# A decode layer on one core: the first MLP layer by wide matmuls on four column strips, gelu and silu by tanh

## The chip, the core and the metric

The kernel runs on one core of a Trainium2 chip. The metric is the device time of one execution in microseconds (us). TensorE is written PE in the profile (PEld for its weight loads), VectorE is DVE, ScalarE is ACT, GpSimd is POOL, and SyncE, which issues most of the DMAs, is SP.

## What is computed

Four batch rows, one token each. The token is layer-normed once; the result goes through attention over the last 1024 positions of a cache (32 query heads, 8 key/value heads, head size 128) and through an MLP with its own layer norm; the two are multiplied, the MLP's output after a silu, and added to the input.

```python
x = A_x                                   # (4, 1, 512)
xn = layernorm(x)
q = xn @ wq                               # 32 heads of 128
s = softmax(q k^T * 128**-0.5) v @ wo     # k, v: last 1024 rows of the caches
y = layernorm(xn)
h = gelu(y @ w1 + b1)                     # tanh form; w1 is (512, 1792)
g = silu(h @ w2 + b2)                     # w2 is (1792, 512)
out = x + s * g
```

All inputs are bf16. With four rows nearly all the work is moving weights and caches: 16 MB of K and V, 4 MB each of `wq` and `wo`, 1.75 MB each of `w1` and `w2`.

## The kernel before

The program is written out as a list of operations for each engine. `_Program.add` (L28) appends an operation with what it depends on to one engine's list, `dma` (L33) does it for a transfer, and `emit` (L52) writes each engine's list in that order, with a semaphore wait ahead of an operation where a dependency lies on another engine. So the order of the `add` calls is the order of each engine's queue, and an operation that waits holds up all that stands behind it on its engine.

The work is staged as follows.

- **Loads.** SP issues everything large in one order: `wq` in two halves with the first K heads between them, all K heads (`load_k`, L206), then V(0), `w1`, V(1), `w2`, V(2) to V(7) (`load_v`, L211), then `wo` in six pieces (L459): three of two heads each, one of one head, and the last head as three quarters and one quarter. V(g) takes the buffer of K(g), so its load waits until the transposes of K(g) are done. The small `x`, `b1`, `b2` go on ACT's queue. POOL builds constants: ones, an identity, selection masks, the mask `negm`, and clears `xT`.
- **Norms and queries.** DVE computes both layer norms. `f_xy` (L348) transposes the two normed inputs to `xT` (padded to 32 columns a chunk) and `yT` (4 columns a chunk). `f_q` (L362) computes the queries with `xT` as the loaded side and `wq` as the moving side: 32 matmuls of 512 columns, four at a time on four strips of 32 columns of PE's array (`tile_position`).
- **K phase.** For each of 32 units (4 per head): `T(n)` (L278) transposes eight 128x128 blocks of K on PE (L284), DVE copies the result to `kt_buf` (L290), and `S(n)` (L293) computes scores with eight narrow matmuls (L303), `LAG` = 8 units later. At the end of a head ACT takes the exponent into `P_buf` (L311).
- **V phase.** For each head `PV(g)` (L315) does 32 matmuls (L321) and one 512-column matmul with ones for the denominator (L327). `epilogue(g)` (L331) reduces and inverts the denominator and scales, on DVE. PV(g) waits for epilogue(g-2).
- **MLP.** It is put between heads by the loop that ends with the calls of `mlp1` to `mlp4`. `mlp1` (L391) follows PV(0): for each of 14 chunks of the hidden size, four matmuls with a block of `w1` as the loaded side (its columns 14 elements apart, L397) and 4 moving columns of `yT`, and one with a row of `b1` (L399). The hidden layer so stands transposed, 128 partitions by 56. ACT squares it (L404), DVE forms the cubic argument (L405, L407), ACT takes an exponent (L408); `mlp2` (L411, called after PV(1)) adds one, inverts and multiplies on DVE to give `hT`. `mlp3` (L418) does the second layer, 56 matmuls with blocks of `w2` as the loaded side (L424) and 4 with a row of `b2` (L426), then an exponent on ACT (L430); `mlp4` (L433, after PV(2)) makes the silu, `g_sb`, on DVE.
- **End.** After the last epilogue, `to_rows` (L462) brings the attention output into the order of `wo`'s rows (L470, L477), `wo(k, rows)` (L483) does 128 matmuls in six groups, one for each piece of `wo`, each waiting for its piece (L491). The sum is multiplied with `g_sb` (L517), transposed (L521), added to `x` (L523) and stored (L525).

Of the kernel before, what the change touches and what calls it, by code (L numbers as in the profile page):

```python
# [16 lines left out]
class _Program:  # L17
# [56 lines left out]
def bass_recurrent_scan__sliding_block_cached__mixer_channel_mlp__decode_kernel(  # L74
# [25 lines left out]
    F = B_w1.shape[1]  # L100
    FC = F // 128
# [6 lines left out]
    NKT = LAG + 2  # L108
    NB = 3
    SCALE = DH ** -0.5  # L110
    GELU_A = 1.5957691216057308
    GELU_K = 0.044715
    EPS = 1e-5
    NEG = -30000.0
# [1 line left out]
    sb = nc.alloc_sbuf_tensor  # L116
# [13 lines left out]
    x32 = sb([4, 512], F32)  # L130
# [5 lines left out]
    xn32 = sb([4, 512], F32)  # L136
    xn_bf = sb([4, 512], BF16)
    st2 = sb([4, 6], F32)
    mv2 = sb([4, 2], F32)
# [5 lines left out]
    ones_bf = sb([128, 128], BF16)  # L145
    ident = sb([128, 128], BF16)
# [4 lines left out]
    negm = sb([128, 512], BF16)  # L151

    xT = sb([128, 4, 32], BF16)
    yT = sb([128, 16], BF16)
    q_sb = sb([128, 2, 512], BF16)
    qT = sb([128, 128], BF16)
    b1_sb = sb([1, F], BF16)
    b2_sb = sb([1, D], BF16)
    sel = sb([128, 4, 32], BF16)
    OW = sb([128, 4, HKV * 4], BF16)  # L160
    hT = sb([128, FC * 4], BF16)

    OTb = sb([128, HKV * 16], BF16)
    den_sb = sb([128, HKV * 16], F32)
    rden = sb([128, HKV * 16], F32)

    u2_sb = sb([128, FC * 4], F32)
    t_sb = sb([128, FC * 4], F32)
    t2_sb = sb([128, FC * 4], F32)
    ge_sb = sb([128, FC * 4], F32)  # L170
    e1_sb = sb([128, FC * 4], F32)
    r_sb = sb([128, FC * 4], F32)

    ez_sb = sb([128, 16], F32)
    d1_sb = sb([128, 16], F32)
    rz_sb = sb([128, 16], F32)
    g_sb = sb([128, 16], F32)
    sg_sb = sb([128, 16], F32)
    o_bf = sb([16, 128], BF16)
# [5 lines left out]
    PS_Q, PS_H, PS_Z, PS_W = 0, 128, 192, 208  # L185

    pg = _Program(nc)
    add = pg.add
# [3 lines left out]
    d_b1 = pg.dma("act", "b1", lambda e: e.dma_start(  # L192
        b1_sb[0:1, :], B_b1.rearrange("(o n) -> o n", o=1)))
    d_b2 = pg.dma("act", "b2", lambda e: e.dma_start(
        b2_sb[0:1, :], B_b2.rearrange("(o n) -> o n", o=1)))

    def cache_rows(cache, g):

# [27 lines left out]
    for g in range(2, HKV):  # L226
# [5 lines left out]
    c_id = add("gp", lambda e: e.affine_select(  # L232
        ident[:, :], ones_bf[:, :], [[1, 128]], ALU.is_equal, 0.0,
        base=0, channel_multiplier=-1), c_1)
# [4 lines left out]
        sel[:, :, :], ones_bf[:, :], [[1, 4], [4, 32]], ALU.is_equal, 0.0,  # L239
        base=0, channel_multiplier=-1), c_1)  # L240
    c_xT = add("gp", lambda e: e.memset(xT[:, :, :], 0.0))
    c_z = add("gp", lambda e: e.memset(zero_bf[:, :], 0.0))
    c_neg = add("gp", lambda e: e.affine_select(
        negm[:, :], zero_bf[:, :], [[0, 32], [1, 4], [0, 4]], ALU.is_equal, NEG,
# [98 lines left out]

    v_xyT = None
# [3 lines left out]
    def f_xy(pe):  # L348
# [35 lines left out]
    for k in range(2):  # L384
        v_q = add("dve", lambda e, k=k: e.tensor_copy(
            bass.AP(qT, k * 64, [[128, 128], [16, 4], [4, 4], [1, 4]]),
            bass.AP(psK[1], k * 512, [[1024, 128], [32, 4], [1, 4], [128, 4]])), t_qT)

    mlp = {}

    def mlp1():  # L391
        def fn(pe):
            last = None
            for k in range(FC):
                o = psM[:, PS_H + k * 4:PS_H + (k + 1) * 4]
                for c in range(4):
                    pe.matmul(o, bass.AP(w1_sb, c * F + k, [[4 * F, 128], [FC, 128]]),  # L397
                              yT[:, c * 4:(c + 1) * 4], start=(c == 0), stop=False)
# [3 lines left out]
        h = psM[:, PS_H:PS_H + FC * 4]  # L402
        t = add("pe", fn, v_xyT, d_w1, d_b1)
        a = add("act", lambda e: e.activation(u2_sb[:, :], h, AF.Square), t)  # L404
        v = add("dve", lambda e: e.tensor_scalar(t_sb[:, :], u2_sb[:, :], GELU_K, 1.0,  # L405
                                                 op0=ALU.mult, op1=ALU.add), a)
        v = add("dve", lambda e: e.tensor_tensor(t2_sb[:, :], t_sb[:, :], h, ALU.mult), v)  # L407
        mlp["e"] = add("act", lambda e: e.activation(ge_sb[:, :], t2_sb[:, :], AF.Exp,  # L408
                                                     scale=-GELU_A), v)

    def mlp2():  # L411
        h = psM[:, PS_H:PS_H + FC * 4]
# [3 lines left out]
        mlp["h"] = add("dve", lambda e: e.tensor_tensor(hT[:, :], h, r_sb[:, :], ALU.mult), v)  # L416

    def mlp3():  # L418
        def fn(pe):
            last = None  # L420
            for c in range(4):
                o = psM[:, PS_Z + c * 4:PS_Z + (c + 1) * 4]
                for k in range(FC):
                    pe.matmul(o, w2_sb[:, k, c * 128:(c + 1) * 128], hT[:, k * 4:(k + 1) * 4],  # L424
                              start=(k == 0), stop=False)
                last = pe.matmul(o, b2_sb[0:1, c * 128:(c + 1) * 128], ones_bf[0:1, 0:4],  # L426
                                 start=False, stop=True)
            return last
        t = add("pe", fn, mlp["h"], d_w2, d_b2)
        mlp["ez"] = add("act", lambda e: e.activation(  # L430
            ez_sb[:, :], psM[:, PS_Z:PS_Z + 16], AF.Exp, scale=-1.0), t)

    def mlp4():  # L433
        v = add("dve", lambda e: e.tensor_single_scalar(d1_sb[:, :], ez_sb[:, :], 1.0, ALU.add),
                mlp["ez"])
        v = add("dve", lambda e: e.reciprocal(rz_sb[:, :], d1_sb[:, :]), v)
        mlp["g"] = add("dve", lambda e: e.tensor_tensor(
            g_sb[:, :], psM[:, PS_Z:PS_Z + 16], rz_sb[:, :], ALU.mult), v)

    NUN = HKV * NU  # L440
    for n in range(LAG, NUN + LAG):
# [137 lines left out]
```

## Time and profile before

| | |
|---|---|
| median of 4 runs | 77.22 us (77.1 to 77.3) |
| the profiled execution's own time | 77.23 us |
| its span in the profile | 75.3 us |
| granted PE clock, mean over the span | 0.803 |
| PE matmuls busy | 52.5 us (70%), 1107 of them |
| PE weight loads busy | 45.3 us (60%) |
| DVE busy | 38.4 us (51%) |
| ACT busy | 9.0 us (12%) |
| read from HBM | 28.85 MB |

The span runs from the first to the last instruction of the profiled execution; the time of a run also has what lies around it. A line of the page's groups names the kernel's line, the engine, the operation, what is written and read with shapes, and how often; then busy time and the mean of one in ns. In the timeline a row has start and length in us, and in square brackets how long the engine stood idle before it and what ended that. In the chain of work that ended last a row has start, length and what it was; "issue" is time in which the engine waited for nothing that the profile shows.

### The profile page before, as it was taken

The page shows a single profiled execution, that of the slowest core. Times are in us where ns is not written, and L with a number is a line of the kernel's source. Part 1 is how long each engine was busy: PE and PEld are TensorE (multiplying, and loading weights), DVE is VectorE, ACT ScalarE, POOL GpSimd, SP SyncE. Part 2 cuts the span into 40 slices and gives each one's busy share as a digit, 9 for nine tenths or more (in the row PEclk, how much of TensorE's full clock was granted, in tenths as well). Part 3 has the DMA queues.
Part 4 walks back from the last instruction along what each step waited for, and adds up shares of the span by engine and source line. Part 5 has one row for each costly group of instructions (what it writes and reads, how often), then busy time and mean ns, then how long its engine had stood idle before and what let it go on. Part 6 is the DMA issues. An engine that isn't in the chain of part 4 may idle for free.

```text
span 75.3 us, 2408 instructions
## 1 busy us (share of the span) xinstructions
PE 52.5 (70%) x1107; PEld 45.3 (60%) x1107; DVE 38.4 (51%) x84; ACT 9.0 (12%) x16; POOL 4.5 (6%) x13
## 2 busy tenths in 40 slices
PE   0000039974789979979968944999839999937960
PEld 0000039963269979969957933999639856806940
DVE  0778006894258979959975100000691687781010
ACT  0611000000270302303201520000200000000000
POOL 6970000000000000000000000000000000000000
PEclk9999999999999999999999996555555555555555
DMA  1899999998999999999999999999999999999600
GB/s 36 270 428 414 420 431 461 461 418 374 431 431 418 418 426 422 431 426 460 428 391 441 438 420 399 418 418 426 422 439 435 409 400 418 429 405 425 249 11 2
DMA packets 4213, 28.99 MB, mean 385 GB/s; under 512 B 486, under 2 KB 619, under 8 KB 1644
## 3 DMA queue, kind: packets, MB, share of 16 engines
q1 hardware_dynamic: 4160, 28.84, 92.1%
q8 instruction: 8, 0.13, 0.6%
q10 hardware_dynamic: 44, 0.01, 0.1%
q14 instruction: 1, 0.01, 0.0%
HBM read 28.85 MB, written 0.00 MB: 383 GB/s over the span
## 4 chain that ended last, share of the span: by engine, by line
DMA 36%; PE 34%; SPq 17%; DVE 5%; issue 4%
DMA wo_sb<-in_A_wo_dram 24%; PE psK L284 21%; SPq L459 16%; DMA kv_buf<-in_A_k_cache_dram 12%; PE psS L303 6%; DVE kt_buf L290 3%; PE psO L367 3%; PE psS L299 2%; DVE q_sb L373 1%; PE psK L379 1%; PE psM L491 1%; PE psK L352 1%; PE psS L521 1%; SPq L219 1%; SPq L212 0%
## 5 line engine op out<-in xcount | busy, mean ns | idle before, releaser
L284 PE MATMUL psK<-ident,kv_buf 128*128 128x128 bf16 x256 | 20.7, 233 | 12.2 <-DMA kv_buf<-in_A_k_cache_dram 10.7
L290 DVE COPY kt_buf<-psK 128x1024 bf16<-128x1024 bf16 x32 | 21.2, 691 | 8.4 <-PE psK L284 8.1
L284 PEld LDWEIGHTS psK<-ident,kv_buf 128*128 128x128 bf16 x256 | 16.6, 105 | 11.8 <-DMA kv_buf<-in_A_k_cache_dram 10.7
L303 PEld LDWEIGHTS psS<-qT,kt_buf 128*128 128x128 bf16 x256 | 9.4, 96 | 2.1 <-issue 1.2
L303 PE MATMUL psS<-qT,kt_buf 128*128 128x16 bf16 x256 | 10.4, 169 | 0.4 <-issue 0.4
L321 PEld LDWEIGHTS psO<-P_buf,kv_buf 128*128 128x128 bf16 x256 | 7.5, 103 | 2.1 <-issue 2.1
L321 PE MATMUL psO<-P_buf,kv_buf 128*128 128x16 bf16 x256 | 8.0, 174 | 0.2
L397 PE MATMUL psM<-yT,w_sb 128*128 128x4 bf16 x56 | 5.7, 204 | 2.1 <-issue 2.1
L311 ACT ACTIVATE P_buf<-psS 128x512 bf16<-128x512 f32 x8 | 4.8, 597 | 16.8 <-PE psS L303 16.8
L334 DVE TENSOR_REDUCE den_sb<-psS 128x16 f32<-128x512 f32 x8 | 5.5, 690 | 1.4 <-PE psS L327 1.2
L405 DVE TENSOR_SCALAR t_sb<-u_sb 128x56 f32<-128x56 f32 x1 | 0.2, 193 | 11.7 <-ACT u_sb L404 11.7
L397 PEld LDWEIGHTS psM<-yT,w_sb 128*128 128x128 bf16 x56 | 4.5, 153 | 2.5 <-issue 2.3
L327 PE MATMUL psS<-P_buf,ones_bf 128*128 128x512 bf16 x8 | 4.5, 561 | 0.0
L491 PE MATMUL psM<-OW,wo_sb 128*128 128x4 bf16 x128 | 3.9, 166 | 0.6 <-DVE OW L477 0.5
L491 PEld LDWEIGHTS psM<-OW,wo_sb 128*128 128x128 bf16 x128 | 3.7, 104 | 0.8 <-issue 0.6
L424 PE MATMUL psM<-hT,w_sb 128*128 128x4 bf16 x56 | 2.1, 167 | 1.4 <-DVE hT L416 1.4
L299 PE MATMUL psS<-negm,ind 128*128 128x512 bf16 x8 | 3.0, 380 | 0.0
L399 PE MATMUL psM<-ones_bf,b_sb 1*128 1x4 bf16 x14 | 3.0, 215 | 0.0
L424 PEld LDWEIGHTS psM<-hT,w_sb 128*128 128x128 bf16 x56 | 1.8, 105 | 1.9 <-DVE hT L416 1.9
L517 DVE TENSOR_TENSOR sg_sb<-psM,g_sb 128x16 f32<-128x16 f32 x1 | 0.2, 184 | 4.1 <-PE psM L491 4.1
L374 ACT ACTIVATE q_sb<-psO 128x512 bf16<-128x512 f32 x1 | 0.6, 597 | 13.5 <-PE psO L367 13.5
L337 DVE RECIPROCAL rden<-den_sb 128x16 f32<-128x16 f32 x8 | 2.0, 253 | 0.3
(63 smaller groups left out, 28.5 us busy)
## 6 DMA issues: line engine op xcount, KB each, us to landing
kv_buf<-in_A_k_cache_dram SPq DMA_DIRECT2D x8, 1024.0 KB, 20.7
kv_buf<-in_A_v_cache_dram SPq DMA_DIRECT2D x8, 1024.0 KB, 23.7
wq_sb<-in_A_wq_dram SPq DMA_DIRECT2D x2, 2048.0 KB, 11.4
w_sb<-in_B_w_dram SPq DMA_DIRECT2D x2, 1792.0 KB, 28.3
wo_sb<-in_A_wo_dram SPq DMA_DIRECT2D x3, 1024.0 KB, 24.8
wo_sb<-in_A_wo_dram SPq DMA_DIRECT2D x1, 512.0 KB, 21.4
wo_sb<-in_A_wo_dram SPq DMA_DIRECT2D x1, 384.0 KB, 18.0
wo_sb<-in_A_wo_dram SPq DMA_DIRECT2D x1, 128.0 KB, 17.9
```

Of the source, the lines that this page charges most:

```text
L284: last = pe.transpose(psK[n % NB][:, j * 128:(j + 1) * 128], kv_buf[:, g, u * UT + j, :], ident[:, :])
L290: cp[n] = add("dve", lambda e: e.tensor_copy(kt_buf[:, n % NKT, :], psK[n % NB][:, 0:1024]), t, sc.get(n - NKT))
L299: pe.matmul(psS[g % 2][:, 0:512], ind[:, :], negm[:, :], start=True, stop=False, skip_group_check=True)
L303: last = pe.matmul(psS[g % 2][:, c * 16:(c + 1) * 16], kt_buf[:, n % NKT, j * 128:(j + 1) * 128], qT[:, g * 16:(g + 1) * 16], start=False, ...
L311: ex[g] = add("act", lambda e: e.activation(P_buf[:, g, :], psS[g % 2][:, 0:512], AF.Exp, scale=SCALE), sc[n])
L321: last = pe.matmul(pso[:, 0:16], kv_buf[:, (HKV + g) % NS, c, :], P_buf[:, g, c * 16:(c + 1) * 16], start=(c == 0), stop=(c == NC - 1))
L327: den[g] = add("pe", lambda pe: pe.matmul(psS[g % 2][:, 0:512], ones_bf[:, :], P_buf[:, g, :], start=True, stop=True), ex[HKV - 2 + g % 2] ...
L334: v = add("dve", lambda e: e.tensor_reduce(den_sb[:, cs], bass.AP(psS[g % 2], 0, [[512, 128], [1, 16], [16, NC]]), AX.X, ALU.add), den[g])
L397: pe.matmul(o, bass.AP(w1_sb, c * F + k, [[4 * F, 128], [FC, 128]]), yT[:, c * 4:(c + 1) * 4], start=(c == 0), stop=False)
L424: pe.matmul(o, w2_sb[:, k, c * 128:(c + 1) * 128], hT[:, k * 4:(k + 1) * 4], start=(k == 0), stop=False)
L459: e.dma_start(wo_sb[:, g0:g1, i0:i1, :], wo_r[:, g0:g1, i0:i1, :]))))
L491: last = pe.matmul(psM[:, PS_W + c * 4:PS_W + (c + 1) * 4], wo_sb[:, g, i, c * 128:(c + 1) * 128], OW[:, i, g * 4:(g + 1) * 4], start=firs ...
```

## The change

The hidden layer is computed in rows instead of columns. `yT` is padded to 32 columns a chunk, like `xT`, and becomes the loaded side; `w1` becomes the moving side. Each of four column strips takes four of the 14 hidden chunks (the first chunks are 0, 4, 8 and 10, so two chunks are computed twice), 512 columns a matmul: 4 x 4 matmuls, and 4 more that add `b1` by a row of ones. The moving side reads `w1` with a step of 14 elements. The result stands in PSUM as 128 partitions (four strips of 32, of which four rows each are used) by 512.

Gelu is taken in its tanh form on tiles of 128x512: a square on ACT, one combined add-and-multiply on DVE, a tanh on ACT, then half of (tanh + 1) and a product on DVE. The tiles lie in buffers of `kt_buf`, which the K phase no longer needs, and the sums in `psK[0]`. Four transposes on PE and one DVE copy with a rearranged order bring it to `hT`.

The second layer is the same 56 blocks, with the loop over hidden chunks outside; its bias is one matmul ahead of them, with `b2` loaded as four rows of 128 and the identity's first four columns repeated four times as the moving side. Silu is taken by tanh too. `epilogue(0)` is moved ahead of `mlp1`. `x32` and `xn32` now lie inside `P_buf`, and POOL clears `yT`.

The core of the diff (declarations of tiles left out):

```diff
-    v_xyT = add("dve", lambda e: e.tensor_copy(yT[:, :], psK[1][:, 16:32]), t_xy)
+    v_xyT = add("dve", lambda e: e.tensor_copy(
+        yT[:, :, 0:4], psK[1][:, 16:32].rearrange("p (c b) -> p c b", c=4)), t_xy, c_yT)
...
+    K0 = (0, 4, 8, FC - 4)
+    def f32k(n):
+        return kt_buf[:, n, :].bitcast(F32)
+    hb = kt_buf[:, 4, 0:512]
+    h_ps = psK[0][:, 0:1024].bitcast(F32)
     def mlp1():
         def fn(pe):
             last = None
-            for k in range(FC):
-                o = psM[:, PS_H + k * 4:PS_H + (k + 1) * 4]
-                for c in range(4):
-                    pe.matmul(o, bass.AP(w1_sb, c * F + k, [[4 * F, 128], [FC, 128]]),
-                              yT[:, c * 4:(c + 1) * 4], start=(c == 0), stop=False)
-                last = pe.matmul(o, bass.AP(b1_sb, k, [[F, 1], [FC, 128]]), ones_bf[0:1, 0:4],
-                                 start=False, stop=True)
+            for c in range(4):
+                for s in range(4):
+                    pe.matmul(psK[0][32 * s:32 * s + 32, 0:1024].bitcast(F32), yT[:, c, :],
+                              bass.AP(w1_sb, c * F + K0[s], [[4 * F, 128], [1, 4], [FC, 128]]),
+                              start=(c == 0), stop=False, tile_position=(0, 32 * s))
+            for s in range(4):
+                last = pe.matmul(psK[0][32 * s:32 * s + 32, 0:1024].bitcast(F32),
+                                 ones_bf[0:1, 0:32],
+                                 bass.AP(b1_sb, K0[s], [[F, 1], [1, 4], [FC, 128]]),
+                                 start=False, stop=True, tile_position=(0, 32 * s))
             return last
...
-        t = add("pe", fn, v_xyT, d_w1, d_b1)
-        a = add("act", lambda e: e.activation(u2_sb[:, :], h, AF.Square), t)
-        v = add("dve", lambda e: e.tensor_scalar(t_sb[:, :], u2_sb[:, :], GELU_K, 1.0,
-                                                 op0=ALU.mult, op1=ALU.add), a)
-        v = add("dve", lambda e: e.tensor_tensor(t2_sb[:, :], t_sb[:, :], h, ALU.mult), v)
-        mlp["e"] = add("act", lambda e: e.activation(ge_sb[:, :], t2_sb[:, :], AF.Exp,
-                                                     scale=-GELU_A), v)
+        t = add("pe", fn, v_xyT, d_w1, d_b1, *[cp[n] for n in range(NUN - NB, NUN)])
+        a = add("act", lambda e: e.activation(f32k(0), h_ps, AF.Square), t)
+        v = add("dve", lambda e: e.scalar_tensor_tensor(f32k(1), f32k(0), 1.0 / GELU_K, h_ps,
+                                                        op0=ALU.add, op1=ALU.mult), a)
+        mlp["t"] = add("act", lambda e: e.activation(f32k(2), f32k(1), AF.Tanh,
+                                                     scale=GELU_C * GELU_K), v)
     def mlp2():
-        v = add("dve", lambda e: e.tensor_single_scalar(e1_sb[:, :], ge_sb[:, :], 1.0, ALU.add),
-                mlp["e"])
-        v = add("dve", lambda e: e.reciprocal(r_sb[:, :], e1_sb[:, :]), v)
-        mlp["h"] = add("dve", lambda e: e.tensor_tensor(hT[:, :], h, r_sb[:, :], ALU.mult), v)
+        v = add("dve", lambda e: e.tensor_scalar(f32k(3), f32k(2), 0.5, 0.5,
+                                                 op0=ALU.mult, op1=ALU.add), mlp["t"])
+        v = add("dve", lambda e: e.tensor_tensor(hb, f32k(3), h_ps, ALU.mult), v)
+        def fn(pe):
+            last = None
+            for t in range(4):
+                last = pe.transpose(psK[2][:, t * 128:(t + 1) * 128],
+                                    kt_buf[:, 4, t * 128:(t + 1) * 128], ident[:, :])
+            return last
+        t = add("pe", fn, v, cp[NUN - 1], cp[NUN - 2])
+        mlp["h"] = add("dve", lambda e: e.tensor_copy(
+            bass.AP(hT, 0, [[64, 128], [4, 16], [1, 4]]),
+            bass.AP(psK[2], 0, [[1024, 128], [32, 16], [1, 4]])), t)
     def mlp3():
         def fn(pe):
-            last = None
-            for c in range(4):
-                o = psM[:, PS_Z + c * 4:PS_Z + (c + 1) * 4]
-                for k in range(FC):
-                    pe.matmul(o, w2_sb[:, k, c * 128:(c + 1) * 128], hT[:, k * 4:(k + 1) * 4],
-                              start=(k == 0), stop=False)
-                last = pe.matmul(o, b2_sb[0:1, c * 128:(c + 1) * 128], ones_bf[0:1, 0:4],
-                                 start=False, stop=True)
+            last = pe.matmul(psM[:, PS_Z:PS_Z + 16], b2_sb[:, :],
+                             bass.AP(ident, 0, [[128, 4], [1, 4], [0, 4]]),
+                             start=True, stop=False, skip_group_check=True)
+            for k in range(FC):
+                s = min(k // 4, 2) if k < FC - 4 else 3
+                n = (k - K0[s]) * 16 + s * 4
+                for c in range(4):
+                    last = pe.matmul(psM[:, PS_Z + c * 4:PS_Z + (c + 1) * 4],
+                                     w2_sb[:, k, c * 128:(c + 1) * 128], hT[:, n:n + 4],
+                                     start=False, stop=(k == FC - 1), skip_group_check=True)
             return last
-        t = add("pe", fn, mlp["h"], d_w2, d_b2)
-        mlp["ez"] = add("act", lambda e: e.activation(
-            ez_sb[:, :], psM[:, PS_Z:PS_Z + 16], AF.Exp, scale=-1.0), t)
+        t = add("pe", fn, mlp["h"], d_w2, d_b2, c_id)
+        mlp["tz"] = add("act", lambda e: e.activation(
+            tz_sb[:, :], psM[:, PS_Z:PS_Z + 16], AF.Tanh, scale=0.5), t)
     def mlp4():
-        v = add("dve", lambda e: e.tensor_single_scalar(d1_sb[:, :], ez_sb[:, :], 1.0, ALU.add),
-                mlp["ez"])
-        v = add("dve", lambda e: e.reciprocal(rz_sb[:, :], d1_sb[:, :]), v)
+        v = add("dve", lambda e: e.tensor_scalar(sz_sb[:, :], tz_sb[:, :], 0.5, 0.5,
+                                                 op0=ALU.mult, op1=ALU.add), mlp["tz"])
...
     for g in range(HKV):
         PV(g)
         if g == 0:
+            epilogue(0)
             mlp1()
-        if g >= 1:
+        if g >= 2:
             epilogue(g - 1)
         if g == 1:
             mlp2()
             mlp3()
         if g == 2:
             mlp4()
```

More of the change, by code (lines that the diff above doesn't have):

```diff
@@ L110, in bass_recurrent_scan__sliding_block_cached__mixer_channel_mlp__decode_kernel @@
     SCALE = DH ** -0.5
-    GELU_A = 1.5957691216057308
+    GELU_C = 0.7978845608028654
     GELU_K = 0.044715
@@ L129, in bass_recurrent_scan__sliding_block_cached__mixer_channel_mlp__decode_kernel @@
     x16 = sb([16, 128], BF16)
-    x32 = sb([4, 512], F32)
+    x32 = P_buf[0:4, 4:6, :].rearrange("p g n -> p (g n)").bitcast(F32)
+    xn32 = P_buf[0:4, 6:8, :].rearrange("p g n -> p (g n)").bitcast(F32)
     st1 = sb([4, 6], F32)
@@ L135, in bass_recurrent_scan__sliding_block_cached__mixer_channel_mlp__decode_kernel @@
     rstd1 = sb([4, 1], F32)
-    xn32 = sb([4, 512], F32)
     xn_bf = sb([4, 512], BF16)
@@ L153, in bass_recurrent_scan__sliding_block_cached__mixer_channel_mlp__decode_kernel @@
     xT = sb([128, 4, 32], BF16)
-    yT = sb([128, 16], BF16)
+    yT = sb([128, 4, 32], BF16)
     q_sb = sb([128, 2, 512], BF16)
@@ L157, in bass_recurrent_scan__sliding_block_cached__mixer_channel_mlp__decode_kernel @@
     b1_sb = sb([1, F], BF16)
-    b2_sb = sb([1, D], BF16)
+    b2_sb = sb([4, 128], BF16)
     sel = sb([128, 4, 32], BF16)
     OW = sb([128, 4, HKV * 4], BF16)
-    hT = sb([128, FC * 4], BF16)
+    hT = sb([128, 64], BF16)
     OTb = sb([128, HKV * 16], BF16)
@@ L165, in bass_recurrent_scan__sliding_block_cached__mixer_channel_mlp__decode_kernel @@
     rden = sb([128, HKV * 16], F32)
[L167 to L176, printed above, removed]
+    tz_sb = sb([128, 16], F32)
+    sz_sb = sb([128, 16], F32)
     g_sb = sb([128, 16], F32)
@@ L184, in bass_recurrent_scan__sliding_block_cached__mixer_channel_mlp__decode_kernel @@
     psM = nc.alloc_psum_tensor("psM", [128, 512], F32)
-    PS_Q, PS_H, PS_Z, PS_W = 0, 128, 192, 208
+    PS_Z, PS_W = 192, 208
     pg = _Program(nc)
@@ L194, in bass_recurrent_scan__sliding_block_cached__mixer_channel_mlp__decode_kernel @@
     d_b2 = pg.dma("act", "b2", lambda e: e.dma_start(
-        b2_sb[0:1, :], B_b2.rearrange("(o n) -> o n", o=1)))
+        b2_sb[:, :], B_b2.rearrange("(c n) -> c n", c=4)))
     def cache_rows(cache, g):
@@ L241, in bass_recurrent_scan__sliding_block_cached__mixer_channel_mlp__decode_kernel @@
     c_xT = add("gp", lambda e: e.memset(xT[:, :, :], 0.0))
+    c_yT = add("gp", lambda e: e.memset(yT[:, :, :], 0.0))
     c_z = add("gp", lambda e: e.memset(zero_bf[:, :], 0.0))
@@ L402, in mlp1 @@
-        h = psM[:, PS_H:PS_H + FC * 4]
-        t = add("pe", fn, v_xyT, d_w1, d_b1)
-        a = add("act", lambda e: e.activation(u2_sb[:, :], h, AF.Square), t)
-        v = add("dve", lambda e: e.tensor_scalar(t_sb[:, :], u2_sb[:, :], GELU_K, 1.0,
-                                                 op0=ALU.mult, op1=ALU.add), a)
-        v = add("dve", lambda e: e.tensor_tensor(t2_sb[:, :], t_sb[:, :], h, ALU.mult), v)
-        mlp["e"] = add("act", lambda e: e.activation(ge_sb[:, :], t2_sb[:, :], AF.Exp,
-                                                     scale=-GELU_A), v)
@@ L411, in mlp2 @@
-    def mlp2():
-        h = psM[:, PS_H:PS_H + FC * 4]
-        v = add("dve", lambda e: e.tensor_single_scalar(e1_sb[:, :], ge_sb[:, :], 1.0, ALU.add),
-                mlp["e"])
-        v = add("dve", lambda e: e.reciprocal(r_sb[:, :], e1_sb[:, :]), v)
-        mlp["h"] = add("dve", lambda e: e.tensor_tensor(hT[:, :], h, r_sb[:, :], ALU.mult), v)
+            for c in range(4):
[3 more added lines that the diff above has]
+                              start=(c == 0), stop=False, tile_position=(0, 32 * s))
@@ L437, in mlp4 @@
         mlp["g"] = add("dve", lambda e: e.tensor_tensor(
-            g_sb[:, :], psM[:, PS_Z:PS_Z + 16], rz_sb[:, :], ALU.mult), v)
+            g_sb[:, :], psM[:, PS_Z:PS_Z + 16], sz_sb[:, :], ALU.mult), v)
     NUN = HKV * NU
```

## The prediction

> **What bounds the kernel now.** I read the page first: slices, then queues.
>
> ```profile
> span 75.3 us, 2408 instructions
> ...
> PEclk9999999999999999999999996555555555555555
> DMA  1899999998999999999999999999999999999600
> ...
> q1 hardware_dynamic: 4160, 28.84, 92.1%
> q8 instruction: 8, 0.13, 0.6%
> ```
>
> The DMA row is at nine tenths from slice 2 until slice 37: 28.84 MB flow without a hole, and that stream alone fills the span until about 72 us. TensorE's clock halves in slice 24 (about 45.5 us) and stays there, so all the work the change touches is priced at half clock. Queue q8 brings instructions: eight packets of 16 KB.
>
> Then the chain of work that ended last (start, length, what):
>
> ```profile
> 26.67 0.45 issue
> ...
> 32.77 0.54 issue
> ...
> 38.91 0.97 issue
> ...
> 53.87 18.02 DMA wo_sb<-in_A_wo_dram
> 71.90 0.05 issue
> 71.94 0.61 PE psM L491 x16
> ```
>
> The end hangs on a transfer: the fifth piece of `wo`, issued at 53.87, lands at 71.90, and its 12 matmuls and the 4 of the last piece (issued at 54.35, 17.9 us to landing, so 72.25) follow. TensorE is barely ahead: in the timeline cut finely, the 112th matmul of L491 starts at 71.73 and the 113th at 71.94, where the row's pace is 0.03. So it waited 0.18 us; that is all its slack. Both bounds meet here: a faster TensorE gains nothing, a slower one costs from 0.18 us on.
>
> Last, the timeline around the MLP:
>
> ```profile
> 46.27 0.34 PE L397 MATMUL psM<-yT,w_sb 128*128 128x4 bf16 x3 [2.10 <-issue]
> ...
> 52.95 1.02 PE L321 MATMUL psO<-P_buf,kv_buf 128*128 128x16 bf16 x32
> ...
> 55.51 0.22 DVE L416 TENSOR_TENSOR hT<-psM,r_sb 128x56 bf16<-128x56 f32 x1
> ...
> 55.78 0.53 PE L424 MATMUL psM<-hT,w_sb 128*128 128x4 bf16 x14 [1.37 <-DVE hT L416]
> ...
> 58.10 1.02 PE L321 MATMUL psO<-P_buf,kv_buf 128*128 128x16 bf16 x32
> ...
> 68.61 3.93 PE L491 MATMUL psM<-OW,wo_sb 128*128 128x4 bf16 x128 [0.51 <-DVE OW L477]
> ```
>
> From its second matmul (46.27) the first layer takes 6.7 us, PV(1) with its denominator 1.5, TensorE then stands 1.37 waiting for `hT`, the second layer takes 2.3, and PV(2) starts at 58.10. From there TensorE is busy nearly throughout (8.27 of 8.50 us from 58.0 to 66.5), so every shift of PV(2) arrives at L491 unless something else is late. That date, 58.10, is what I track.
>
> The "issue" gaps need an explanation, since one of them (2.1 us) lies at the start of `mlp1`. Counting TensorE's loads, matmuls and waits, the gaps before 27.11, 33.31, 39.88 and 46.27 stand exactly 256 instructions apart, each 16 KB packet (0.13 MB in 8) is then 256 instructions of 64 bytes, and the restarts are 6.2, 6.6 and 6.4 us apart. I read them as TensorE waiting for its next 256 instructions. The next three such borders (in L424, PV(4), L491) show no stall before the change, with TensorE slower than 256 in 6.4 us.
>
> **What the Trainium skill says.** "TensorE: Matmul & The Clock Gate", Part 3, says that matmuls on different column strips run side by side. The trace agrees: in the chain the 32 wide matmuls of L367 take 1.94 us, 8 rounds of four at 0.21 and a tail, and a lone 512-column L299 also adds 0.22. "SBUF — State Buffer", section Door 1: The DMA port swizzle, says that reads which jump to a new 16-byte line at each element pay a penalty. The trace agrees for weight loads: L397, stepping 28 bytes, spaces loads 60 ns apart (4 in 0.32), L424, contiguous, 27 ns (14 in 0.45). For a moving operand no row shows it. "ScalarE: Activation LUTs", Table sets, puts exp and tanh in one set; if so no load is added (the trace's loads cost 1.28 us each, and it has no tanh).
>
> **The change part by part.**
>
> *First layer.* It removes 56+14 narrow matmuls (6.7 us) and adds 16+4 of 512 columns on four strips: five rounds. The half-clock round is 0.43 us: L327 with 512 columns goes from 0.38 at full clock to 0.59, so half a round is 0.21. Low bound: 5 x 0.43 + 0.2 latency = 2.3 us. But the moving side steps 28 bytes. If each strip's stream reads at the pace of the strided loads (60 ns for 32 columns of each of four streams, 1.88 ns an element), a round is 0.96 and the layer 5.0. If strips don't overlap at all: 20 x 0.43 + 0.2 = 8.8. I take 5.0, the nearest row's pace; 2.3 and 8.8 stay as ends. The 2.1 us gap ahead stays, since TensorE's program is the same up to it. The weights landed at 40.9 (issued 14.9, 26.0 to landing), so they aren't waited for.
>
> *Gelu chain.* Tiles grow from 128x56 to 128x512. Square 0.60 (L311's and L374's ACT of this size), multiply-add from PSUM 0.69 (L334, L373; a slower form could add 0.5), tanh 0.60, scale by a half 0.60 (L260, 512 f32; could be half), product from PSUM 0.69, four transposes about 0.5 (L284: 8 in 0.46 at full clock, twice as long at half, with a tail), copy 0.22 (L385), seven handovers at 0.04: 4.2 us (3.6 to 4.9). Before it was 2.7. PV(1) and its denominator (1.5) lie inside it; the rest, 2.7, is TensorE standing at the transposes, with the second layer and all PV behind them. Epilogue(0) is moved ahead of `mlp1`, so it no longer stands in VectorE's queue within this chain; epilogue(1) now follows the `hT` copy, beside the second layer, and PV(3), which needs it, comes later.
>
> *Second layer.* 57 matmuls for 60, contiguous weights: 57 x 27 ns + 0.2 = 1.75 for 2.3. The bias by one matmul is within it.
>
> *Silu by tanh.* One VectorE operation fewer of 0.25; off the path, as `g` was ready at 59.1 and is needed at 68.6.
>
> *Start.* One more POOL memset (0.20, like L241) ahead of `negm`, which is done by 4.75 and needed at 22; the `b2` load in four rows stays a small one on ACT's queue; SP's queue and all large transfers are untouched, and V's loads wait only for K's transposes, which don't change. So the landing dates stay, 71.90 and 72.25.
>
> *Sum.* PV(2) starts at 46.27 + 5.0 + 4.2 + 1.75 = 57.2, 0.9 earlier (3.6 earlier with 2.3; 2.9 later with 8.8). At the other end 71.90 doesn't move: 16 matmuls, 72.54, tail to 75.3. Saved on the path: nothing. The 0.9 is turned into waiting for `wo`.
>
> *Instruction borders.* TensorE's program is 97 shorter (100 fewer in the first layer, 6 fewer in the second, 9 more for transposes and their wait), so the next borders fall 27 instructions into PV(2), 15 into PV(6), and after 52 matmuls of L491. With PV(2) at 57.2 the first is passed at 57.6; at 6.4 us a packet the second opens at 64.0 where PV(6) gets there at 63.1, the third at 70.4 where L491 gets there at about 70.15; the remaining 76 matmuls then end 0.2 later than now. At the pace of the late borders before (4.9 us from L424's to PV(4)'s at most) nothing is lost.
>
> The profiled run took 77.23 for a span of 75.3, so 1.93 lies outside; its time stands at the median of the runs, 77.22. Forecast: 75.3 + 1.93 = **77.2 us, no change**.
>
> **Rivals.**
> A (forecast), 77.2: `wo`'s landing sets the end in both. For it: the 18 us DMA link in the chain and the 0.18 us wait.
> B, slower, 77.6: with a first layer at 5 us or somewhat over, instruction packets hold TensorE at PV(6) and in L491: 0.2 as worked out, up to 0.8 if the chain is at its upper end. Against: no stall at the three late borders.
> C, slower, 79.9: strided streams on four strips don't overlap; first layer 8.8, PV(2) 2.9 late, less 0.18. It decides from a first layer of 6.1 us (58.28 - 46.27 - 5.95). For it: the strided loads' 60 against 27 ns. Against: L367's strips do overlap.
> D, faster, 77.0: the wide matmuls bring the full clock back and it lasts to the end. The skill's clock-gate page (Part 1) ties the clock to TensorE's activity. 16 matmuls at 22.5 ns (L303's pace, 8 in 0.18) for 29.5 save 0.11, and the f32 transpose of L521 at most the 0.21 of a 512-column pass: 0.2 to 0.3. Against: the page's half clock holds through nearly full TensorE work, and L491 will stand waiting.
>
> **How the numbers follow.** A 0.56, B 0.17, C 0.08, D 0.19. A measurement of this kernel can tell about 0.2% (0.15 us; the runs span 77.1 to 77.3) from no change. Of A I count 0.43 within that, 0.09 faster (the near tie of two bounds dissolves), 0.04 slower; with B, C and D: faster 0.28, same 0.43, slower 0.29. The range goes from D's better half, 76.9, through B to 78.0, leaving C and a little of D out. A alone: 77.05 to 77.35.
>
> **What would show it.** Right: L491 starts earlier but stands in gaps before its last 64, 32, 16 and 4 matmuls, and the chain ends again with a `wo` transfer near 71.9. The first layer's size shows in the rows of its wide matmuls: rounds 0.43, 0.96 or 1.7 us apart. B shows as "issue" gaps in PV(6) and L491, C as an unbroken L491 that ends after 72.6, D as PEclk above 5 in the last slices. Wrong: any `wo` landing that moves by over 0.15 us, or a table load ahead of tanh.

## The result, and the profile after

The changed kernel takes 76.94 us (median of 44 executions, 76.79 to 77.38); the kernel before, measured beside it, 77.08 us (63 executions, 76.86 to 77.73). The ratio is 0.9976 with a 95% interval of 0.9967 to 0.9985: faster by a quarter of a per cent, where no change was forecast. The spread tells more than the medians. Of the kernel before, 19 of 63 executions took over 77.2 us; of the changed one, 1 of 44. The lower quarters of the two are 76.97 and 76.88, the upper quarters 77.26 and 77.02. What the change took away is mostly the upper tail.

The ratios in this document leave out executions over 1.5% above the fastest of their kernel; for the versions that are slowed below, these are the very ones that count, so their times are given as well.

The page of the changed kernel (its profiled execution took 76.87 us, span 75.2):

```profile
span 75.2 us, 2309 instructions
...
PEclk9999999999999999999999999559855555555555
DMA  1999999998999999999999999999999999999600
...
q1 hardware_dynamic: 4160, 28.84, 92.2%
```

The DMA row is the same solid block with the same 28.84 MB. TensorE's clock comes back for two slices after the wide matmuls and is at half again long before the end.

The timeline of its TensorE, from the first layer on (start, length in us, what, idle time before it):

```profile
46.60 3.81 PE L400 MATMUL psK<-w_sb,yT 128*32 128x512 bf16 x15 [0.83 <-issue]
47.49 0.14 PEld L400 LDWEIGHTS psK<-w_sb,yT 128*32 128x32 bf16 x4 [0.77 <-issue]
48.40 0.13 PEld L400 LDWEIGHTS psK<-w_sb,yT 128*32 128x32 bf16 x3 [0.78 <-issue]
...
51.35 0.96 PE L315 MATMUL psO<-P_buf,kv_buf 128*128 128x16 bf16 x32
...
54.69 0.61 PE L424 MATMUL psK<-ident,kt_buf 128*128 128x128 bf16 x4 [2.14 <-DVE kt_buf L419]
...
57.22 1.00 PE L315 MATMUL psO<-P_buf,kv_buf 128*128 128x16 bf16 x32
...
67.71 1.55 PE L507 MATMUL psM<-OW,wo_sb 128*128 128x4 bf16 x53 [0.51 <-DVE OW L493]
69.85 1.72 PE L507 MATMUL psM<-OW,wo_sb 128*128 128x4 bf16 x59 [0.58 <-issue]
...
71.80 0.59 PE L507 MATMUL psM<-OW,wo_sb 128*128 128x4 bf16 x16 [0.24 <-DMA wo_sb<-in_A_wo_dram]
```

PV(2) starts at 57.22, 0.9 earlier than before. The last layer begins at 67.71, also 0.9 earlier, stands 0.58 for instructions after 53 matmuls and then waits openly for a `wo` transfer. The chain of the same run (start, length, what) ends where the chain before did:

```profile
53.63 18.13 DMA wo_sb<-in_A_wo_dram
71.76 0.05 issue
71.80 0.60 PE psM L507 x16
```

The two profiled executions took 77.23 and 76.87 us, 0.36 apart. The landing, 71.76 for 71.90, is 0.14 of that, and the two traces' spans, 75.31 and 75.15, are 0.16 apart. The other 0.2 us lie outside the span (1.92 and 1.72), where neither the landing nor TensorE's last layer reaches. One execution can't tell whether any of this is the cause.

### The profile page after: what moved, and what is told of

It is laid out like the page before. It is cut to its first block, busy times and chain, and to the rows that moved or that the text cites. A ratio compares the mean times of both kernels' runs of the same rounds, so it can differ in the third digit from the quotient of the medians.

```text
span 75.2 us, 2309 instructions
## 1 busy us (share of the span) xinstructions
PE 52.0 (69%) x1058; PEld 40.1 (53%) x1058; DVE 39.5 (53%) x82; ACT 9.8 (13%) x16; POOL 4.6 (6%) x14
## 3 DMA queue, kind: packets, MB, share of 16 engines
q1 hardware_dynamic: 4160, 28.84, 92.2%
## 4 chain that ended last, share of the span: by engine, by line
PE 37%; DMA 36%; SPq 16%; issue 4%; DVE 3%
DMA wo_sb<-in_A_wo_dram 24%; PE psK L278 23%; SPq L475 15%; DMA kv_buf<-in_A_k_cache_dram 12%; PE psS L297 6%; PE psO L362 3%; PE psS L293 2%; DVE kt_buf L284 2%; DVE q_sb L368 1%; PE psK L374 1%; PE psM L507 1%; PE psK L346 1%; PE psS L538 1%; SPq L212 1%; SPq L205 0%
## 5 line engine op out<-in xcount | busy, mean ns | idle before, releaser
L278 PE MATMUL psK<-ident,kv_buf 128*128 128x128 bf16 x256 | 21.5, 239 | 11.7 <-DMA kv_buf<-in_A_k_cache_dram 10.5
L278 PEld LDWEIGHTS psK<-ident,kv_buf 128*128 128x128 bf16 x256 | 17.4, 109 | 11.3 <-DMA kv_buf<-in_A_k_cache_dram 10.5
L400 PE MATMUL psK<-w_sb,yT 128*32 128x512 bf16 x16 | 4.9, 1084 | 0.8 <-issue 0.8
L411 DVE SCALAR_TENSOR_TENSOR kt_buf<-kt_buf,psK 128x512 f32<-128x512 f32 x1 | 0.7, 689 | 6.1 <-ACT kt_buf L410 6.1
L400 PEld LDWEIGHTS psK<-w_sb,yT 128*32 128x32 bf16 x16 | 0.5, 108 | 3.6 <-issue 3.6
L246 DVE CAST P_buf<-x_bf 4x512 f32<-4x512 bf16 x1 | 0.9, 910 | 2.3 <-DMA x_bf<-in_A_x_dram 2.3
L424 PE MATMUL psK<-ident,kt_buf 128*128 128x128 bf16 x4 | 0.6, 308 | 2.1 <-DVE kt_buf L419 2.1
L362 PE MATMUL psO<-wq_sb,xT 128*32 128x512 bf16 x32 | 1.9, 380 | 0.3 <-DVE xT L351 0.3
```

What stands on the lines that cost most here:

```text
L278: last = pe.transpose(psK[n % NB][:, j * 128:(j + 1) * 128], kv_buf[:, g, u * UT + j, :], ident[:, :])
L362: last = pe.matmul(psO[m // 4][32 * s:32 * s + 32, 0:512], xT[:, c, :], wq_sb[:, c, m * 512:(m + 1) * 512], start=(c == 0), stop=(c == 3), ...
L400: pe.matmul(psK[0][32 * s:32 * s + 32, 0:1024].bitcast(F32), yT[:, c, :], bass.AP(w1_sb, c * F + K0[s], [[4 * F, 128], [1, 4], [FC, 128]]) ...
```

## The experiments

**Two theories.** T, a near tie: TensorE's lead over the last `wo` pieces is not the 0.18 us of one profile but varies between executions, so that the kernel before ends late in some. S, a small load: in the first profiles the last of the 16 landings of each large transfer trails the others by about 0.15 us before and not after, from about 10.6 us on, and again in the last pieces (the last one lands at 72.23 for 72.07); the change loads `b2` as four rows instead of one, and a one-row load might make one DMA engine late for good.

**Small loads, on both sides.** First only the load, in the kernel before; its four bias matmuls stay:

```diff
-        b2_sb[0:1, :], B_b2.rearrange("(o n) -> o n", o=1)))
+        b2_sb[:, :], B_b2.rearrange("(c n) -> c n", c=4)))
...
-                last = pe.matmul(o, b2_sb[0:1, c * 128:(c + 1) * 128], ones_bf[0:1, 0:4],
+                last = pe.matmul(o, b2_sb[:, :], bass.AP(ident, c, [[128, 4], [0, 4]]),
```

> The kernel before with b2 loaded as four rows of 128 instead of one row of 512, and its four bias matmuls taken from the four rows; TensorE has the same number of instructions. Theory S (small load): the one-row b2 load makes one DMA engine about 0.16 us late in the first 8 us, that engine stays late, and its share of the last wo pieces sets the end. Then the time falls to the changed kernel's, ratio to before 0.998, and the last of the 16 landings of each large transfer loses its 0.15 us lead over the second last. Theory T (near tie): before, TensorE is in many executions not quite ahead of the last wo pieces. Then nothing changes, ratio 1.000.

Measured: 77.04 us against 77.14, ratio 0.9979 (0.9955 to 1.0004), 14 executions from 76.93 to 77.45, 1 of them over 77.2 where 24 of the 59 beside it were. T had forecast 1.000, S 0.998; the interval holds both, and the short tail speaks against T. Alone that settles nothing. Then the reverse, the changed kernel with `b2` in one row (its load and tile as in the kernel before, left out here):

```diff
-            last = pe.matmul(psM[:, PS_Z:PS_Z + 16], b2_sb[:, :],
-                             bass.AP(ident, 0, [[128, 4], [1, 4], [0, 4]]),
-                             start=True, stop=False, skip_group_check=True)
+            for c in range(4):
+                last = pe.matmul(psM[:, PS_Z + c * 4:PS_Z + (c + 1) * 4],
+                                 b2_sb[0:1, c * 128:(c + 1) * 128], ones_bf[0:1, 0:4],
+                                 start=(c == 0), stop=False, skip_group_check=True)
```

> The changed kernel with b2 loaded in one row again and four bias matmuls in the second layer. S: the gain is gone, ratio to before 1.000, and one landing of each transfer is late by 0.15 us again. T: the gain stays, ratio 0.998, since TensorE is still about 0.6 us early.

77.02 us, ratio 0.998 (0.9965 to 0.9996), none of 22 executions over 77.2: the gain stays. Next, more of the suspected cause, and less of it, both in the changed kernel. First four more one-row loads (`mlp4` then waits for them too, left out here):

```diff
+        d_xb.append(pg.dma("act", "xb%d" % i, lambda e, i=i: e.dma_start(
+            xb[0:1, i * 800:(i + 1) * 800], B_b1.rearrange("(o n) -> o n", o=1)[:, 0:800])))
```

> The changed kernel with four more one-row loads of 1.6 KB at the start, into a tile that nobody reads. S: the engine that carries them becomes later by some 0.3 us, one of the 16 landings of every large transfer shows it up to the last wo piece, and the time rises by 0.2 to 0.3 us, ratio to before 1.000 to 1.002. T: no change, 0.998.

Then `b1` in 16 runs:

```diff
-        b1_sb[0:1, :], B_b1.rearrange("(o n) -> o n", o=1)))
+        b1_sb[0:1, :].rearrange("o (a n) -> o a n", a=16),
+        B_b1.rearrange("(o a n) -> o a n", o=1, a=16)))
```

> The changed kernel with b1 loaded as 16 runs of 112 instead of one of 1792. S (a small load that falls on one DMA engine makes it late to the end): a little faster than the changed kernel, ratio to before 0.997. T: as the changed kernel, 0.998.

With four more loads: ratio 0.9976 (0.996 to 0.9991), and the last piece landed at 72.04, not later. With `b1` spread: 0.9978 (0.9962 to 0.9993), last piece at 72.20. S falls as it was put: neither one row of `b2` nor four further one-row loads cost the gain, and the four made nothing later. Whether the four-row load alone gains something in the kernel before, 14 executions don't show.

**TensorE early, in the kernel before.** Its 14 matmuls with `b1` are left out, so the first layer lacks its bias:

```diff
-                              yT[:, c * 4:(c + 1) * 4], start=(c == 0), stop=False)
-                last = pe.matmul(o, bass.AP(b1_sb, k, [[F, 1], [FC, 128]]), ones_bf[0:1, 0:4],
-                                 start=False, stop=True)
+                              yT[:, c * 4:(c + 1) * 4], start=(c == 0), stop=(c == 3))
```

> The kernel before without the 14 matmuls that add b1 (the bias of the first layer is left out), which makes TensorE some 2 us earlier at PV(2) and changes no load. S: ratio 1.000. T: TensorE is clear of the wo pieces, ratio 0.998.

77.02 us, ratio 0.9977 (0.9962 to 0.9992), 1 of 22 over 77.2. None of the change is in this kernel, and it has the whole gain. The lead is larger than expected: its first layer takes 3.3 us (44.98 to 48.30) for 6.7. But TensorE's program is also 28 instructions shorter, so this run alone doesn't show that the lead is what counts. Its last layer shows the floor:

```profile
67.29 1.02 PE L489 MATMUL psM<-OW,wo_sb 128*128 128x4 bf16 x32 [0.40 <-DMA wo_sb<-in_A_wo_dram]
69.79 1.01 PE L489 MATMUL psM<-OW,wo_sb 128*128 128x4 bf16 x32 [1.49 <-DMA wo_sb<-in_A_wo_dram]
71.03 0.59 PE L489 MATMUL psM<-OW,wo_sb 128*128 128x4 bf16 x16 [0.23 <-DMA wo_sb<-in_A_wo_dram]
71.97 0.60 PE L489 MATMUL psM<-OW,wo_sb 128*128 128x4 bf16 x16 [0.35 <-DMA wo_sb<-in_A_wo_dram]
```

Each group stands until its piece of `wo` is in; in these four rows 2.5 us of lead are waited away. With `b2` in four rows on top (the same bias left out):

> The kernel before with b2 in four rows and without the 14 matmuls that add b1 (the first layer's bias is left out): the small load spread and TensorE 2 us early. If S and T each hold a part of the gain, this is faster than the run without the 14 matmuls alone, ratio 0.997 for 0.998. With T alone 0.998, the same as that run.

Ratio 0.9975 (0.996 to 0.999), the same.

**The same kernels again.** For second profiles, both unchanged.

> The kernel before, unchanged, for a second profile. T: TensorE's stalls before the MLP and the date at which it reaches the last matmuls differ from the first profile by 0.5 us or more, and the landings of wo by less than 0.15. Ratio 1.000.

> The changed kernel, unchanged, for a second profile and beside the others on one chip: ratio 0.998, upper quarter of its times below that of before by 0.2 us, lower quarter by less than 0.1.

Before again: 77.29 us, ratio 1.0012 (0.9985 to 1.0039), 14 executions from 76.98 to 77.99, 10 of them over 77.2. After again: 77.03, ratio 0.9976 (0.996 to 0.9991), 22 executions from 76.86 to 77.18. The second profile of before took 77.26, its chain of work reads:

```profile
68.23 0.30 DVE OW L477
68.67 3.85 PE psM L491 x128
72.54 0.20 DVE sg_sb L517
```

No `wo` transfer is in it: the 128 matmuls run through, and TensorE is what ends last. So the same kernel is bound by `wo` in one execution and by TensorE in another. That is not why this one took 77.26, though: its span is 75.3 as in the first profile, and its last DVE operation starts at 73.20 where that one's starts at 73.24. The changed kernel's second profile, 76.94 us, is bound by TensorE too, with the border's stall on the path:

```profile
68.03 1.55 PE psM L507 x53
69.59 0.57 issue
70.16 2.30 PE psM L507 x75
```

So the change didn't make every execution wait for `wo`. The forecast for the second profile of before was a difference of 0.5 us or more in TensorE's stalls and date. That missed: PV(2) starts at 58.16 for 58.10, the last layer at 68.67 for 68.61, and the stalls ahead of the first layer sum to 4.2 for 4.1.

Other profiles show that TensorE's date can move much more than that. In the kernel with only `b2`'s load changed, whose TensorE does the work of before, the instruction stalls ahead of the first layer are these:

```profile
37.80 0.38 PE L284 MATMUL psK<-ident,kv_buf 128*128 128x128 bf16 x4 [0.51 <-issue]
43.64 0.34 PE L397 MATMUL psM<-yT,w_sb 128*128 128x4 bf16 x3 [1.56 <-issue]
```

That is 2.1 us, and PV(2) starts at 55.47. Before again it has these:

```profile
27.71 0.29 PE L303 MATMUL psS<-qT,kt_buf 128*128 128x16 bf16 x6 [1.10 <-issue]
33.64 0.22 PE L284 MATMUL psK<-ident,kv_buf 128*128 128x128 bf16 x1 [0.27 <-issue]
40.48 0.38 PE L284 MATMUL psK<-ident,kv_buf 128*128 128x128 bf16 x4 [1.24 <-issue]
46.33 0.34 PE L397 MATMUL psM<-yT,w_sb 128*128 128x4 bf16 x3 [1.56 <-issue]
```

That is 4.2 us, and PV(2) starts at 58.16. The last piece of `wo` landed at 72.09 and 72.19 in the two. TensorE's date differs by 2.7 us, 2.1 of it in these stalls, the transfer's by 0.1. These two kernels differ in a small load. But two versions of the changed kernel that come below, one with contiguous reads and one with two more matmuls, have the same loads and the same TensorE program up to the first layer. They ran on one chip, and PV(0) starts at 41.61 in the profile of the one and at 43.70 in that of the other. So the date varies by 2 us without any change ahead of it.

**TensorE late.** Matmuls of 512 columns whose result is unused are put ahead of the second layer: two in the changed kernel, two in the kernel before, four in the changed one.

```diff
+            for _ in range(2):
+                pe.matmul(psK[1][:, 0:1024].bitcast(F32), ones_bf[:, :], P_buf[:, 0, :],
+                          start=True, stop=True)
```

> The changed kernel with two more 512-column matmuls (result unused) ahead of the second layer, 0.86 us at half clock, so that PV(2) starts at about the kernel before's 58.1. S: the gain stays, ratio 0.998, the end moves by 0.1 us at most. T: the gain is gone, ratio 1.000.

> The kernel before with two more 512-column matmuls (result unused) ahead of the second layer, 0.86 us at half clock: PV(2) would start at about 59.0 in an execution with the stalls of the profiled one. T, now with a cause: the instruction stalls of TensorE in the K phase vary by some 2 us between executions, so its lead over the last wo pieces varies as much; with 0.86 us less lead most executions end late, median ratio to before 1.005 to 1.010, some still at 77.0. S: 0.86 less 0.18 of slack in all executions, ratio 1.009 with a narrow spread.

> The changed kernel with four such matmuls, 1.7 us: PV(2) at about 58.9, the same date as in the kernel before with two. T: only that date counts, so the same ratio as there, 1.005 to 1.010. If the changed kernel had another advantage (loads, tail), it would stay faster than that run.

| | median | range | executions over 77.5 | ratio |
|---|---|---|---|---|
| changed, two more | 76.99 | 76.84 to 77.91 | 2 of 14 | 0.9989 (0.9962 to 1.0016) |
| before, two more | 77.16 | 76.89 to 78.85 | 7 of 22 | 0.9986 (0.9966 to 1.0006) |
| changed, four more | 77.72 | 76.94 to 79.0 | 8 of 14 | 1.0007 (0.9969 to 1.0045) |

What T forecast in kind came: less lead leaves the lower end at 76.9 and grows an upper tail. S's narrow shift of all executions did not come. In the two profiled executions of the changed kernel that ended late (77.91 us with two more, 78.03 with four) the chain holds no `wo` transfer, and the spans are 76.2 and 76.3. The medians came out otherwise than forecast. For the first row T had said 1.000, and the interval holds that as well as 0.998. For the middle row I had given 1.005 and more; two thirds of these executions still stayed under 77.5. The last two rows were to be equal. Their medians are not, but 7 late executions of 22 and 8 of 14 are too few to tell the rows apart. If they do differ, the profiled execution of the third (78.03 us) shows one possible reason:

```profile
69.21 1.45 PE L510 MATMUL psM<-OW,wo_sb 128*128 128x4 bf16 x49 [0.51 <-DVE OW L496]
71.29 2.25 PE L510 MATMUL psM<-OW,wo_sb 128*128 128x4 bf16 x79 [0.63 <-issue]
```

The changed kernel's program has an instruction border inside the last layer, with a stall of 0.6 us there; the profile of before with two more has no stall in that place.

**Inside the span and outside it.** The time of an execution is its span and what lies around it. Both are on record for every execution of these runs. The means in us, over the executions that the ratios use (spans are recorded to 0.1 us):

| | executions | time | span | outside |
|---|---|---|---|---|
| before, beside the first four experiments | 59 | 77.20 | 75.35 | 1.85 |
| before without the `b1` matmuls | 22 | 77.02 | 75.26 | 1.76 |
| before, `b2` in four rows | 14 | 77.07 | 75.27 | 1.80 |
| changed, `b2` in one row | 22 | 77.03 | 75.26 | 1.77 |
| changed, two more matmuls | 14 | 77.07 | 75.33 | 1.74 |
| before, beside the second profiles | 55 | 77.22 | 75.36 | 1.86 |
| changed, again | 22 | 77.02 | 75.25 | 1.77 |
| before, two more matmuls | 17 | 77.15 | 75.32 | 1.83 |
| changed, four more matmuls | 10 | 77.38 | 75.64 | 1.74 |

About half of the gain lies in the span: 0.11 of 0.20 us from before to changed in the second set. There T fits. Spans of 75.4 and more are 19 of 59 in the kernel before and 1 of 22 without the `b1` matmuls, and in the slowed kernels they come back: 8 of 22 in the kernel before with two more matmuls, 10 of 14 in the changed one with four. The other half, 0.09 us, lies outside the span. T doesn't explain it: in the changed kernel TensorE can be slowed by two or four matmuls, and the time outside stays at 1.74. Nor is the tail over 77.2 all of one kind: 9 of the 24 such executions in the first row have a span of 75.3 or less.

What makes the time outside shorter stays open; the traces hold nothing of it. One order is on record. The pages of all versions with 1.80 us and more outside count 2408 instructions or more, and those of all versions with 1.77 and less count 2380 or fewer. No run separates that from the rest, and leaving out the `b1` matmuls moves both the lead and this count.

**The first layer at contiguous pace.** The changed kernel with its moving reads of `w1` and `b1` contiguous; the hidden units then stand in another order than the rows of `w2`:

```diff
-                              bass.AP(w1_sb, c * F + K0[s], [[4 * F, 128], [1, 4], [FC, 128]]),
+                              bass.AP(w1_sb, c * F + K0[s] * 128, [[4 * F, 128], [1, 512]]),
...
-                                 bass.AP(b1_sb, K0[s], [[F, 1], [1, 4], [FC, 128]]),
+                                 bass.AP(b1_sb, K0[s] * 128, [[F, 1], [1, 512]]),
```

> The changed kernel whose moving reads of w1 and b1 run through 512 neighbouring columns instead of stepping 14 (so hidden units stand in another order than the rows of w2 they meet). If the step is what slows the wide matmuls, rounds of four fall from 0.91 us to 0.43 and PV(2) starts some 2.3 us earlier than the changed kernel's 57.2. Both theories, S and T: the time stays at the changed kernel's, ratio to before 0.998, since the wo pieces set the end.

```profile
44.63 1.90 PE L400 MATMUL psK<-w_sb,yT 128*32 128x512 bf16 x15 [1.51 <-issue]
46.46 0.61 PE L404 MATMUL psK<-b_sb,ones_bf 1*32 1x512 bf16 x4
47.00 1.03 PE L315 MATMUL psO<-P_buf,kv_buf 128*128 128x16 bf16 x32
```

From the stall to PV(1) the layer takes 2.4 us instead of 4.8 (46.60 to 51.35): the step of 28 bytes doubles its time. The time is 76.99 us, ratio 0.9973 (0.9955 to 0.999), none of 22 over 77.2: on the floor, like the others. A first layer twice as fast buys nothing measurable over the changed kernel.

**Moving the floor.** Last, the landing itself, with TensorE's program as in the changed kernel: the last piece of `wo`, then the last two, as transfers of 8 rows.

```diff
...
+                e.dma_start(wo_sb[p:p + 8, g0:g1, i0:i1, :], wo_r[p:p + 8, g0:g1, i0:i1, :])
+                for p in range(0, 128, 8)])
...
```

> The changed kernel with the last piece of wo (128 KB) issued as sixteen transfers of 8 rows instead of one of 128, so that it goes through 8 of the 16 DMA engines. Under the theory that the landing of wo is the floor for every version with TensorE early: if those 8 are engines that carried no instruction packet and finish at 70.4, the piece lands before the piece ahead of it (71.8), and the time falls by about 0.1 us, ratio to before 0.996; if they are the late ones, it lands about 1 us later and the ratio is 1.01. If the floor were elsewhere (the tail, the start), nothing changes: 0.998.

> The same for the last two pieces (512 KB in 32 transfers). If the 8 engines are the early ones, both pieces are in by about 71.5, ratio 0.993; if they are the late ones, about 74, ratio 1.03. Without a floor at wo: 0.998.

80.0 us (ratio 1.0356, 1.0313 to 1.04) and 82.72 (1.0707, 1.0667 to 1.0746). The chain of the first:

```profile
64.47 10.75 DMA wo_sb<-in_A_wo_dram
75.22 0.05 issue
75.26 0.28 PE psM L516 x4
```

The last piece lands at 75.22 where it landed at 72.07, 3.1 us later, and the time rises by 3.1. So a later landing of `wo` costs its full delay, by a run that moved it and not by reading alone. In the second the last piece lands at 78.0. No run brought the landing forward, so what an earlier one would gain is not shown. As a way to a faster kernel it failed, and by three times what I had reckoned for the bad case (1 us). No version that I tried has a median below the changed kernel's.

## Why the prediction was wrong, step by step

- **First layer, 5.0 us.** Measured 4.8, from 46.60 to 51.35. The round of four strips was put at 0.96 from the strided weight loads; the loads of one round and the next stand at 46.60, 47.49 and 48.40, so it is 0.91. The strips do run side by side, and the layer is far from the 8.8 us of rival C; C is out. With contiguous reads the low bound of 2.3 came as 2.4.
- **Gelu chain, 4.2 us.** From PV(1)'s start to the second layer at 55.59, 4.2. The scale by a half took 0.43 and not 0.60, the transposes 0.61 and not 0.5.
- **Tanh without a table load.** The Trainium skill, "ScalarE: Activation LUTs", section Table sets, puts exp and tanh in one set. The trace agrees: its two table loads, 1.28 us each, start at 1.91 and 21.30, and ACT's two rows of the chain stand with nothing but DVE's part between them:

```profile
51.47 0.60 ACT L410 ACTIVATE kt_buf<-psK 128x512 f32<-128x512 f32 x1 [7.11 <-PE psK L404]
52.82 0.63 ACT L413 ACTIVATE kt_buf<-kt_buf 128x512 f32<-128x512 f32 x1 [0.76 <-DVE kt_buf L411]
```

- **Second layer, 1.75 us.** 1.6, from 55.59 to 57.2. **PV(2)** was forecast for 57.2 and started at 57.22. That the sum is so exact is luck: the layer began 0.33 later than the 46.27 it starts from, and the two layers were shorter by 0.25 and 0.12. In the second profile it started at 57.54.
- **Instruction borders.** The one in the last layer was put after 52 matmuls and stands after 53, with 0.58 us of stall. The one in PV(6) shows none. Rival B's cost exists. In the first profile it lies under the wait for `wo`; in the second, with 0.57 us, it is on the path.
- **The signs.** The chain ends with a `wo` transfer at 71.76, as forecast. Of the four gaps forecast for the last layer only the one before the last 16 matmuls is there.
- **Rival D.** The full clock did come back (slices 27 and 28), but not to the end: the transpose of the tail takes 0.38 as before. The size of the gain was near D's; its cause was not.
- **The sum, where it failed.** Two of its terms were wrong. The first is "Saved on the path: nothing", from "a faster TensorE gains nothing, a slower one costs from 0.18 us on". That takes the 0.18 us of one profile for the slack of every execution. The gap was there in that execution; in the second profile of the same kernel TensorE was the bound. The prediction had itself traced the "issue" gaps to instruction packets; it used their lengths as fixed. The runs show TensorE's date differing by 2 us between executions with the same program up to there. Lead is therefore worth something in those executions in which TensorE was late, and the mean span falls by about 0.1 us. "The near tie of two bounds dissolves" stood among the cases with a chance of 0.09; it is what happened inside the span, in part: the changed kernel's second profile is still bound by TensorE. The second term is "75.3 + 1.93". It carries the time outside the span over from one execution as if the change couldn't touch it, and gives no reason. In the two profiles of before it is 1.92 and 1.99, in those of the changed kernel 1.72 and 1.72; the means are 1.86 and 1.77. That is the other half of the gain, and its cause stays open.

What stays open besides: the lower quarters, where TensorE should be early in both kernels, still differ by 0.09 us. That is about what the changed kernel's own median differs between two sets of runs (76.94 and 77.03), so I put no cause to it. Why the stalls differ between executions was not tried.

## What to carry to other kernels

Slack between two bounds that meet is a property of an execution, not of a kernel. Where a profile shows one engine a few tenths of a microsecond ahead of a transfer, look at the spread of the times and at a second profile before calling a saving worthless: in the executions that end late, lead is worth something. Once that tail is gone, further lead is worth nothing measurable: the changed kernel with 0.9 us of it and the versions with over 3 us end alike. And before explaining a tail, split each time into its span and the rest. Here half of the difference lay where no line of a profile could show its cause.

## What was not expected of the hardware

- Four 512-column matmuls side by side on four strips take 0.91 us when their moving side steps 28 bytes and 0.43 when it is contiguous, at half clock. The stepped round from 46.60 to 47.49, with a mean granted clock of 0.87, took 0.89, so the full clock didn't help it. L404, whose moving side is a single row of `b1`, slows as much as L400: its matmuls are 1068 ns long, L400's 1084.
- In the first profile of the changed kernel the 16 landings of the last `wo` piece fall in two groups: 8 from 70.39 to 70.64 and 8 from 71.40 to 72.07. The late ones appear one by one during the run, none at 24.9 us, one at 27.3, two at 32.2, five at 45.7, and the instruction packets come in the same rhythm (the first five start at 25.7, 32.0, 38.2, 44.3 and 50.3). If each landing is that of one engine, half of the engines idle for over 1 us at the end while the rest finish. That, and that the packets make them late, is argued from this order and not shown by a run.
- Sixteen transfers of 8 rows took the last 128 KB from landing at 72.1 to landing at 75.2. The trace has nine landings for each of them where it has 16 for a transfer of 128 rows.
